# A planner in place of hand-set rates for the first two stages, and 32x32 squares turned by VectorE

## The chip, the cores and the metric

One core of a Trainium2 chip runs the whole program. The metric is the device time of one execution in microseconds (us). The engines are TensorE (PE, its weight loads PEld), VectorE (DVE), ScalarE (ACT), GpSimd (POOL, unused here) and SyncE (SP), whose queue issues every DMA.

## What is computed

```python
scale = 1.0 / np.sqrt(D)                                   # B, H, S, D = 8, 8, 512, 64; 32 state rows
a  = softmax(scale * x @ state.T);  xread = a  @ state     # per batch and head
a2 = softmax(scale * state @ x.T);  sread = a2 @ x
x = concat([xread, sread], rows).reshape(4352, 512)        # heads side by side
h = ((x @ w1) * (x @ w2)) @ w3 @ w_out                     # 512 -> 1024 -> 1024 -> 512
h = h @ w_in; out = (h - tanh(h)) @ w_out2                 # 512 -> 2048 -> 512
```

The weights come as 64-bit floats and are unpacked on the chip; a product is made of three passes over operands split in a high and a low half.

## The kernel before

A block is one batch: 512 tokens. Blocks 0 to 7 are `xread`, block 8 holds the 256 `sread` rows of all batches. There are four stages, and attention beside the first two.

- **Weights** (`startup`, L551, and what it calls). `w3` and `w_out` are loaded and unpacked: ScalarE makes two instructions of a piece (L153, L154), VectorE three (L161 to L170). `w3` is turned on TensorE (`w_ps`), split (`w3t`) and multiplied with `w_out` into `w3o` (L540). `w1` and `w2` are unpacked in four pairs (`w12_pair`, tiles `raw`, `dt`, `w`).
- **Fold** (L613). The state of four batches times a pair of `w1`, `w2` gives `m`: 16 folds for each half of the batches. ScalarE copies it to `fe`, which goes to DRAM (`mdr`); `load_m` (L648) fetches it block by block as `mq`, and `unfold` (L658) splits it on ScalarE and VectorE into `m`. So stage 1 multiplies the softmax `at` with `m` and needs no `xread`.
- **Attention** (`attn_steps`, L299), for each block: `x` is loaded row by row (`xn`, L293), turned on TensorE in four groups of four 128x128 transposes (`xt_ps`) and copied by ScalarE; scores (L314) are made for tiles of 64 rows; they are turned again (`sm_ps`) so that the 32 scores of a row lie side by side for the first softmax, and after it a third time (`at_ps`). The second softmax goes through `et_ps` and the `sr` matmuls (L379).
- **Stage 1** (L667): two groups `ab_ps` of six matmuls for each of 8 slices k, whose product is split into `ph`. **Stage 2** (L700): `y_ps` adds up over k and goes to DRAM.
- **Stages 3 and 4** (from L846) read `y` back and are left as they are.

The order of the work is written out by hand: a loop over (b, k) calls stage 1 two slices ahead of stage 2, and after each call `point()` (L202) adds parts of attention, folds and unpacking at rates such as 0.58 or 0.5 a call; the start has its own table of digits, `STARTUP` (L37). Every engine runs its instructions in the order in which they were written. PSUM has four work banks in turn, one pool tag `ps`.

Of the kernel before, what the change touches and what calls it, by code (L numbers as in the profile page):

```python
# [18 lines left out]
P = 128  # L19
# [24 lines left out]
def tile_kernel(  # L44
# [31 lines left out]
    pw = ctx.enter_context(tc.tile_pool(name="pw", bufs=4, space=PSUM))  # L76
# [16 lines left out]
        (r, kk): dram.tile([2, 4 * P, 512], F32, name=f"mdr{r}_{kk}")  # L93
# [7 lines left out]
    def ps(name):  # L101
        return pw.tile([P, 512], F32, tag="ps", name=name)
# [56 lines left out]
    def unpack_vector(t):  # L159
        tf = t.bitcast(F32)  # L160
        nc.vector.tensor_scalar(  # L161
            out=tf, in0=tf, scalar1=EXP_LO, scalar2=EXP_HI, op0=ALU.max, op1=ALU.min
        )
        nc.vector.tensor_scalar(
            out=t, in0=t, scalar1=3, scalar2=0x3FFFFFFF,
            op0=ALU.logical_shift_left, op1=ALU.bitwise_and,
        )

    def unpack_end(raw, t):
# [4 lines left out]
        return t.bitcast(F32)  # L174


    jobs = []

    def background():
        if jobs and next(jobs[0], True):  # L180
            jobs.pop(0)

    def drain():
        while jobs:
            background()

    owed = {"major": 0.0, "job": 0.0, "fold": 0.0}
    rate = dict(owed)

    def pay(major, fold, job):  # L190
        for _ in range(major):
            if turned[0] <= limit[0]:
                todo.major()
                todo.minor()
        for _ in range(fold):
            if folds:
                folds.pop(0)()
                settle()
        for _ in range(job):
            background()  # L200

    def point():  # L202

        settle()
        todo.minor()
        due = []
        for k in ("major", "fold", "job"):
            owed[k] += rate[k]
            due.append(int(owed[k] + 1e-6))
            owed[k] -= due[-1]  # L210
        pay(*due)

    folds = []

    turned, limit = [0], [1]

    class Stream:


        def __init__(self, parts):  # L220
            self.parts, self.mark = parts, None
            self.move()

        def move(self):
            self.mark = next(self.parts, None)

        def minor(self):
            if self.mark is False:
                self.move()

        def major(self):
            while self.mark is False:
                self.move()
            settle()
            if self.mark:
                self.move()

        def until(self, seen, key):
            while key not in seen:
                self.major()  # L240
# [17 lines left out]
    with ExitStack() as actx:  # L258
# [18 lines left out]

        def turn_state(r):
# [18 lines left out]


        def attn_steps(b):  # L299
            s = {}  # L300
            bb = b % 4

            def xt(q):
                t = ps(f"xt_ps{b}_{q}")
                transposes(t, [xn[b][:, c, q * P:(q + 1) * P] for c in range(NC)])
                s["xt", q] = pt.tile([P, 512], F32, tag="xt", name=f"xt{b}_{q}", bufs=4)
                copy(s["xt", q], t)

# [22 lines left out]
            def soft(g):
                t = ps(f"sm_ps{b}_{g}")
                sc = s["sc", g]
                transposes(t, [sc[:, c * P:(c + 1) * P] for c in range(NC)])
                r2 = pt.tile([P, 1], F32, tag="r2", name=f"r2{b}_{g}", bufs=2)
                nc.scalar.activation(sc, sc, AF.Exp, bias=s["m2", g], scale=SCALE, accum_out=r2)
                t3 = t.rearrange("p (a n) -> p a n", n=NS)
                na = 512 // NS
                m = pt.tile([P, na], F32, tag="m1", name=f"m1{b}_{g}", bufs=2)
                nc.vector.tensor_reduce(out=m, in_=t3, axis=AX.X, op=ALU.max)  # L340
                a = pt.tile([P, na, NS], F32, tag="xt", name=f"a{b}_{g}", bufs=4)
# [642 lines left out]
```

## Time and profile before

| | |
|---|---|
| median of 3 runs | 1408.23 us (1404.87 to 1409.86) |
| profiled execution | 1408.06 us, its span 1406.2 us |
| TensorE busy | 1312.6 us, 93% |
| VectorE busy | 943.7 us, 67% |
| ScalarE busy | 787.1 us, 56% |
| mean granted TensorE clock | 0.971 |
| DMA | 124.87 MB, 28.6% of 16 engines |

The span runs from the first to the last instruction; 1.9 us lie around it. Shares are means over stages that differ, so the rows below are cut by stretch. A releaser is who ended a wait. Matmuls overlap, so the step from one start to the next says more than a duration.

### The profile page before, as it was taken

The page shows a single profiled execution, that of the slowest core. Times are in us where ns is not written, and L with a number is a line of the kernel's source. Part 1 is how long each engine was busy: PE and PEld are TensorE (multiplying, and loading weights), DVE is VectorE, ACT ScalarE, POOL GpSimd, SP SyncE. Part 2 cuts the span into 40 slices and gives each one's busy share as a digit, 9 for nine tenths or more (in the row PEclk, how much of TensorE's full clock was granted, in tenths as well). Part 3 has the DMA queues.
Part 4 walks back from the last instruction along what each step waited for, and adds up shares of the span by engine and source line. Part 5 has one row for each costly group of instructions (what it writes and reads, how often), then busy time and mean ns, then how long its engine had stood idle before and what let it go on. Part 6 is the DMA issues. An engine that isn't in the chain of part 4 may idle for free.

```text
span 1406.2 us, 17414 instructions
## 1 busy us (share of the span) xinstructions
PE 1312.6 (93%) x6608; PEld 1058.3 (75%) x6608; DVE 943.7 (67%) x1573; ACT 787.1 (56%) x1269; POOL 0.7 (0%) x6
## 2 busy tenths in 40 slices
PE   5865798999899899999999999999999999999997
PEld 3653576767677687987888888888888888888886
DVE  6674445564566655246998768777687776877776
ACT  8956645677665654245655545455454544545454
POOL 0000000000000000000000000000000000000000
PEclk9987799999999999999999999999999999999999
DMA  9717344477765631134301010010100101001000
GB/s 301 244 61 209 90 123 140 136 225 241 209 187 146 183 105 53 53 128 138 117 0 61 0 42 19 1 61 0 60 0 1 60 1 60 0 1 45 1 31 16
DMA packets 92780, 124.87 MB, mean 89 GB/s; under 512 B 41240, under 2 KB 54552, under 8 KB 90648
## 3 DMA queue, kind: packets, MB, share of 16 engines
q1 hardware_dynamic: 92696, 123.76, 28.6%
q8 instruction: 52, 0.85, 0.3%
q14 instruction: 32, 0.26, 0.1%
HBM read 80.74 MB, written 42.99 MB: 88 GB/s over the span
## 4 chain that ended last, share of the span: by engine, by line
PE 72%; ACT 10%; DVE 9%; DMA 4%; issue 2%; SPq 2%; ACTq 0%; DVEq 0%
PE o_ps L903 25%; PE h_ps L141 24%; PE ab_ps L141 11%; PE y_ps L708 9%; DMA mdr<-fe 2%; ACT raw_p L154 1%; ACT fe L111 1%; SPq L632 1%; DMA raw_p<-in_moe_w_dram 1%; ACT raw_w L154 1%; PE m_ps L622 1%; DMA ydr<-y 1%; DVE a L343 1%; DVE m L114 1%; PE sr_ps L379 1%
## 5 line engine op out<-in xcount | busy, mean ns | idle before, releaser
L141 PE MATMUL h_ps<-yt,w2in 128*128 128x512 f32 (+1 forms) x1728 | 394.0, 377 | 0.0
L141 PEld LDWEIGHTS h_ps<-yt,w2in 128*128 128x128 f32 x1728 | 313.4, 188 | 61.2
L141 PE MATMUL ab_ps<-at,m 128*128 128x512 f32 x768 | 213.2, 413 | 25.5 <-ACT m L111 18.1
L708 PE MATMUL y_ps<-ph,w3o 128*128 128x512 f32 (+1 forms) x864 | 218.6, 390 | 0.0
L141 PEld LDWEIGHTS ab_ps<-at,m 128*128 128x128 f32 x768 | 143.4, 195 | 68.6 <-ACT m L111 21.4
L708 PEld LDWEIGHTS y_ps<-ph,w3o 128*128 128x128 f32 x864 | 155.6, 191 | 34.6 <-issue 4.6
L111 ACT ACTIVATE ph<-ac 128x512 fp32r<-128x512 f32 (+1 forms) x72 | 43.8, 609 | 131.7 <-DVE ac L695 131.7
L114 DVE TENSOR_TENSOR m<-mq,m 128x512 fp32r<-128x512 f32 x64 | 44.2, 690 | 83.2 <-ACT m L111 83.2
L114 DVE TENSOR_TENSOR ph<-ac,ph 128x512 fp32r<-128x512 f32 (+1 forms) x72 | 47.7, 663 | 48.7 <-ACT ph L111 48.7
L695 DVE TENSOR_TENSOR ac<-ab_ps,ac 128x512 f32<-128x512 f32 (+1 forms) x72 | 47.4, 658 | 45.2 <-PE ab_ps L141 45.1
L111 ACT ACTIVATE ac<-ab_ps 128x512 f32<-128x512 f32 (+1 forms) x72 | 42.3, 587 | 34.8 <-PE ab_ps L141 30.1
L540 PE MATMUL w3o_ps<-wo,w3t 128*128 128x512 f32 x192 | 55.6, 443 | 5.0 <-ACT w3t L111 3.4
L622 PE MATMUL m_ps<-w,uu 64*128 64x512 f32 x192 | 39.2, 515 | 14.3 <-ACT w L111 5.9
L540 PEld LDWEIGHTS w3o_ps<-wo,w3t 128*128 128x128 f32 x192 | 39.8, 216 | 15.1 <-ACT w3t L111 3.9
L111 ACT ACTIVATE fe<-m_ps 128x512 f32<-128x512 f32 x64 | 34.8, 599 | 23.5 <-DMA mdr<-fe 15.8
L154 ACT ACTIVATE raw_w<-raw_w 128x512 uint16<-128x512 uint32 x32 | 43.7, 1364 | 1.0
L622 PEld LDWEIGHTS m_ps<-w,uu 64*128 64x128 f32 x192 | 22.5, 233 | 28.4 <-ACT w L111 6.5
L111 ACT ACTIVATE m<-mq 128x512 fp32r<-128x512 f32 x64 | 40.8, 637 | 0.0
L133 PE MATMUL w_ps<-ident,dt_p 128*128 128x128 f32 x64 | 12.0, 318 | 30.1 <-DVE dt_p L170 30.1
L913 DVE COPY ob<-o_ps 128x512 f32<-128x512 f32 x17 | 11.8, 692 | 38.6 <-PE o_ps L903 38.6
L111 ACT ACTIVATE ob<-o_ps 128x512 f32<-128x512 f32 x17 | 10.2, 599 | 44.9 <-PE o_ps L903 44.9
L133 PEld LDWEIGHTS w_ps<-ident,dt_p 128*128 128x128 f32 x64 | 8.2, 159 | 34.5 <-issue 23.5
(1812 smaller groups left out, 2353.8 us busy)
## 6 DMA issues: line engine op xcount, KB each, us to landing
mdr<-fe SPq DMA_DIRECT2D x128, 128.0 KB, 2.5
mq<-mdr SPq DMA_DIRECT2D x64, 256.0 KB, 4.5
xn<-in_x_dram SPq DMA_DIRECT2D x32, 256.0 KB, 5.0
raw<-in_moe_w_dram SPq DMA_DIRECT2D x16, 512.0 KB, 8.6
ydr<-y SPq DMA_DIRECT2D x32, 256.0 KB, 3.5
raw_w<-in_moe_w_in_dram SPq DMA_DIRECT2D x16, 512.0 KB, 4.5
raw_w<-in_moe_w_out_dram SPq DMA_DIRECT2D x16, 512.0 KB, 4.2
yr<-ydr SPq DMA_DIRECT2D x8, 1024.0 KB, 4.8
```

The source lines that it names most:

```text
L111: nc.scalar.activation(dst, src, AF.Copy)
L114: nc.vector.tensor_tensor(out=lo, in0=src, in1=hi.bitcast(F32), op=ALU.subtract)
L133: nc.tensor.transpose(dst[:, i * P:(i + 1) * P], s, ident)
L141: nc.tensor.matmul(out_ap, lhs(i), rhs(j), start=(n == 0), stop=(n == m - 1))
L154: nc.scalar.activation(tail, w[:, :, 0], AF.Copy, scale=TAIL)
L343: nc.vector.tensor_tensor(out=a, in0=t3, in1=mb, op=ALU.subtract)
L379: nc.tensor.matmul(t[q * NS:(q + 1) * NS], s["e2t", j][:, c, q * NS:(q + 1) * NS], xn[b][:, c, h * D:(h + 1) * D], start=(c == 0), stop=(c ...
L540: nc.tensor.matmul(acc[a], v[:, i, a * P:(a + 1) * P], wo[j // 2][:, l, (j % 2) * 512:(j % 2) * 512 + 512], start=(j == 0 and e == 0), sto ...
L622: nc.tensor.matmul(ts[j].rearrange("p (k f) -> p k f", k=2), uu[r][d, i, q * P:(q + 1) * P], w[d, :, l, q, :], start=(n == 0), stop=(n == ...
L695: nc.vector.tensor_tensor(out=pf, in0=t, in1=pf, op=ALU.mult)
L708: nc.tensor.matmul(acc[o][:, :n], w3o[k // 2][:, i, c + o * P:c + (o + 1) * P], p[:, j], start=(k == 0 and e == 0), stop=(k == NK - 1 and ...
L903: nc.tensor.matmul(acc[t], g[:, i, t * P:(t + 1) * P], w[:, l, c], start=(f == 0 and e == 0), stop=(f == NF - 1 and e == 2),)
```

## The change

All of the work up to stage 2 is cut into parts. A part names its engine, an estimated duration, what it needs, what it makes, and which slots of which ring it takes and gives. `Plan.run` goes through streams of parts and writes the part that can start first, or one of better rank within 250 ns of it; so the order of every queue comes from the plan. The digits, rates, `point`, `pay` and the generator of attention go. The four PSUM banks get a tag each, which the plan picks. What the parts do changes at these places:

- `x` is loaded a second time as `xb`, in eight DMAs of 32 rows, laid out by head; VectorE turns its 32x32 squares into `xt` (four instructions a block). The state is loaded a second time too (`zb`) and turned the same way (`ut`). Scores are made of tiles of 32 rows, twice as many, adding up in pairs. `by_head` turns the scores in squares in place of `sm_ps`, `back` turns them back in place of `at_ps`. `et_ps` stays on TensorE.
- Folds: for blocks 0 to 3 ScalarE copies one half and VectorE the other; for blocks 4 to 7 the high and the low half are made at the fold and both stored, so `m` is loaded whole, without a split.
- `load_m` takes four DMAs of 32 rows; the ring `m` has three slots, `mq` is gone.

```diff
-STARTUP = (
-    "0000000000010101010101011011011011",
-    "0000000000000000122222222222222222",
-)
+class Plan:
+    NEAR = 250.0
+    REACH = {"PE": 200.0, "ACT": 130.0, "DVE": 130.0, "SP": 0.0}
...
+    def emit(self, p, t):
+        end = t + p["dur"]
+        self.free[p["eng"]] = end
+        if p["bytes"]:
+            self.moved = max(self.moved, t + 600) + p["bytes"] / 300.0
+            end = self.moved + 1600
+        reach = end + self.REACH[p["eng"]]
...
+            t0, _, _, _, p0 = min(can, key=lambda c: c[0])
+            t, _, parts, k, p = min(
+                (c for c in can if c[4]["eng"] == p0["eng"] and c[0] <= t0 + self.NEAR),
+                key=lambda c: (c[1], c[0]),
+            )
+            del parts[k]
+            self.emit(p, t)
...
+        def band(q, j):
+            q = (q + 2 * j) % KT
+            return slice(q * NS, (q + 1) * NS)
...
+        def load_xb(b):
+            if b < B:
+                xb[b] = pt.tile([P, G, 4, NC, D], F32, tag="xb", name=f"xb{b}")
+                for j in range(G):
+                    for q in range(KT):
+                        nc.sync.dma_start(
+                            xb[b][band(q, j), j].rearrange("p g c d -> p g (c d)"),
+                            x[b, 2 * q + j].rearrange("(g p c) d -> p g (c d)", p=NS, c=NC),
+                        )
...
-            def xt(q):
-                t = ps(f"xt_ps{b}_{q}")
-                transposes(t, [xn[b][:, c, q * P:(q + 1) * P] for c in range(NC)])
-                s["xt", q] = pt.tile([P, 512], F32, tag="xt", name=f"xt{b}_{q}", bufs=4)
-                copy(s["xt", q], t)
+            def xt(j, e):
+                t = pt.tile([P, 512], F32, tag="xt", name=f"xt{b}_{j}{e}", bufs=4)
+                nc.vector.transpose(
+                    out=t.rearrange("p (c g i) -> p g c i", c=NC, g=4),
+                    in_=xb[b][:, j, :, :, e * NS:(e + 1) * NS],
+                )
...
+                for e in range(2):
+                    for q in range(KT):
+                        for j in range(G):
+                            d = band(q, j)
+                            nc.tensor.matmul(
+                                s["ps", j][q * NS:(q + 1) * NS],
+                                ut[b // 4][d, j, bb, e], s["xt", j, e][d],
+                                start=(e == 0), stop=(e == 1), tile_position=(d.start, q * NS),
+                            )
...
+            def by_head(j):
+                s["a", j] = pt.tile([P, 512], F32, tag="xt", name=f"a{b}_{j}", bufs=4)
+                nc.vector.transpose(out=s["a", j], in_=s["sc", j])
...
+            def back(j):
+                s["at", j] = pt.tile([P, 512], F32, tag="sc", name=f"at{b}_{j}", bufs=2)
+                nc.vector.transpose(out=s["at", j], in_=s["a", j])
...
+        def fold_whole(kk, q, j):
+            src, f = fold_half(0, kk, q, j, 1)
+            if j == 0:
+                copy(f, src)
+            else:
+                nc.vector.tensor_copy(f, src)
...
-                    mq[b, k] = pa.tile([P, 512], F32, tag="mq", name=f"mq{b}_{k}", bufs=3)
-                    nc.sync.dma_start(mq[b, k], mdr[r, k // 2][k % 2, bb * P:(bb + 1) * P])
+            mt[b, k] = pa.tile([P, 2, 512], F32R, tag="m", name=f"m{b}_{k}", bufs=3)
+            for q in range(KT):
+                rows = slice(q * NS, (q + 1) * NS)
+                to = mt[b, k][rows].bitcast(F32)
+                of = mdr[r, k // 2][q, bb * NS:(bb + 1) * NS, k % 2]
+                nc.sync.dma_start(*((to, of) if r else (to[:, 1], of[:, 1])))
```

How the order moves, at three places. In a name like `ab_ps5_2_0_4143` stand block, slice k, half and a buffer number.

TensorE where block 5 starts stage 1 (`xt`, `et` and `sc` belong to the attention of block 6), before:

```order
L708 MATMUL y_ps4_2_3643<-ph4_5_3843,w3o1_183 128x512 x3
L708 MATMUL y_ps4_3_3647<-ph4_5_3843,w3o1_183 128x512 x3
L141 MATMUL ab_ps5_0_0_3984<-at5_3879,m5_0_3958 128x512 x6
L133 MATMUL xt_ps6_0_3993<-ident_74,xn6_3526 128x128 x4
L708 MATMUL y_ps4_0_3610<-ph4_6_3921,w3o1_183 128x512 x3
L708 MATMUL y_ps4_1_3614<-ph4_6_3921,w3o1_183 128x512 x3
L141 MATMUL ab_ps5_0_1_4014<-at5_3879,m5_0_3958 128x512 x6
L133 MATMUL xt_ps6_1_4025<-ident_74,xn6_3526 128x128 x4
```

and after:

```order
L249 MATMUL ab_ps5_1_1_4130<-at5_3992,m5_1_3783 128x512 x6
L249 MATMUL ab_ps5_2_0_4143<-at5_3992,m5_2_3808 128x512 x6
L249 MATMUL ab_ps5_2_1_4162<-at5_3992,m5_2_3808 128x512 x6
L249 MATMUL ab_ps5_3_0_4177<-at5_3992,m5_3_4089 128x512 x6
L241 MATMUL et_ps6_0_4193<-ident_74,sc6_0_4137 128x128 x4
L249 MATMUL ab_ps5_3_1_4201<-at5_3992,m5_3_4089 128x512 x6
L1035 MATMUL y_ps5_0_4219<-ph5_0_4096,w3o0_525 128x512 x3
L1035 MATMUL y_ps5_1_4223<-ph5_0_4096,w3o0_525 128x512 x3
```

The `xt`, `sm` and `at` groups are gone from between the groups of stages 1 and 2, and several slices of stage 1 now follow one another before stage 2 takes them up.

ScalarE ahead of the first half of `m` (block 0, slice 0), in the weights' part; `fe` are copies of folds, `dt12` and `raw12` the unpacking of `w1` and `w2`. Before:

```order
L111 ACTIVATE at0_845<-at_ps0_1_928 128x512
L153 ACTIVATE dt12_2_0_848<-raw12_4_679 128x512
L154 ACTIVATE raw12_4_679<-raw12_4_679 128x512
L111 ACTIVATE fe0_1_0_946<-m_ps0_1_0_0_938 128x2x256
L111 ACTIVATE fe0_1_0_946<-m_ps0_1_0_1_939 128x2x256
L111 ACTIVATE fe0_1_1_962<-m_ps0_1_1_0_954 128x2x256
L111 ACTIVATE fe0_1_1_962<-m_ps0_1_1_1_955 128x2x256
L111 ACTIVATE fe0_1_2_977<-m_ps0_1_2_0_969 128x2x256
L111 ACTIVATE fe0_1_2_977<-m_ps0_1_2_1_970 128x2x256
L111 ACTIVATE fe0_1_3_992<-m_ps0_1_3_0_984 128x2x256
L111 ACTIVATE fe0_1_3_992<-m_ps0_1_3_1_985 128x2x256
L111 ACTIVATE m0_0_999<-mq0_0_921 128x512
```

and after:

```order
L260 ACTIVATE dt12_4_917<-raw12_4_734 128x512
L265 ACTIVATE raw12_4_734<-raw12_4_734 128x512
L219 ACTIVATE w3o1_940<-w3o_ps1_0_546 128x512
L219 ACTIVATE fe0_1_001_943<-m_ps0_1_0_0_922 128x512
L219 ACTIVATE fe0_1_101_955<-m_ps0_1_1_0_947 128x512
L219 ACTIVATE w3o1_940<-w3o_ps1_1_550 128x512
L219 ACTIVATE m0_0_934<-m0_0_934 128x512
```

Of the second pair's folds two copies stand ahead of it now, not eight, and half of `w3o` comes after it.

SP's queue around the fourth load of block 5 (`raw_w2` fetches and `w2dr` stores belong to the last weights, `ydr` stores to stage 2, `xn` to block 7 or 6), before:

```order
L656 DMA mq5_2_3973<-mdr1_1_99 128x512
L147 DMA raw_w2_27_4009<-in_moe2_w_out_dram 128x1024
L656 DMA mq5_3_4032<-mdr1_1_99 128x512
L756 DMA w2dr_in6_114<-dt_w2_25_3981 128x512
L293 DMA xn7_4057<-in_x_dram 128x8x64
```

and after:

```order
L1049 DMA ydr4_89<-y4_1_4026 128x512
L382 DMA xn6_4031<-in_x_dram 128x8x64 x4
L1141 DMA w2dr_in5_112<-dt_w2_21_3893 128x512
L1049 DMA ydr4_89<-y4_2_4042 128x512
L255 DMA raw_w2_23_4059<-in_moe2_w_out_dram 128x1024
L1049 DMA ydr4_89<-y4_3_4047 128x512
L982 DMA m5_3_4089<-mdr1_1_99 32x1024 x4
L391 DMA xb7_4120<-in_x_dram 32x4x256 x8
L982 DMA m5_4_4154<-mdr1_2_100 32x1024 x4
```

A load is now four DMAs of 32 rows, and the second copy of `x` is eight more between two loads.

## Rows read from the trace of the kernel before

**Rows 1.** The page: busy time of an engine, and the DMA queue's packets, MB, share.

```profile
PE 1312.6 (93%) x6608; PEld 1058.3 (75%) x6608; DVE 943.7 (67%) x1573; ACT 787.1 (56%) x1269; POOL 0.7 (0%) x6
...
q1 hardware_dynamic: 92696, 123.76, 28.6%
```

**Rows 2.** Stretches: us, each engine's busy time (instructions), PEclk, DMA share, GB/s.

```profile
0.00:131.00 131.00, 83.42 (x430) 62.07 (x431) 80.14 (x139) 101.49 (x126) 0.70 (x6) 0.88 0.69 211
131.00:209.00 78.00, 64.43 (x336) 46.17 (x336) 39.95 (x75) 44.33 (x76) 0.00 (x0) 0.84 0.41 105
209.00:652.00 443.00, 422.38 (x2486) 333.25 (x2484) 235.14 (x437) 252.29 (x431) 0.00 (x0) 0.98 0.50 149
652.00:1406.00 754.00, 742.41 (x3360) 616.81 (x3358) 588.45 (x924) 388.96 (x637) 0.00 (x0) 1.00 0.09 31
```

**Rows 3.** Who TensorE waited for: total us, times, longest; 0:131, 131:652, 400:560.

```profile
PE w_ps L133 <- DVE dt_p L170: 30.1, 11, 7.3
...
PE m_ps L622 <- ACT w L111: 5.9, 2, 5.5
...
PE ab_ps L141 <- ACT m L111: 7.9, 3, 4.7
```

**Rows 4.** TensorE in order of time: start, us, instructions, [idle before <-releaser].

```profile
130.67 4.90 PE L141 MATMUL ab_ps<-at,m 128*128 128x512 f32 x12 [2.77 <-ACT m L111]
...
429.03 2.93 PE L141 MATMUL ab_ps<-at,m 128*128 128x512 f32 x6 [2.82 <-ACT m L111]
434.32 1.92 PE L141 MATMUL ab_ps<-at,m 128*128 128x512 f32 x6
...
488.40 2.93 PE L141 MATMUL ab_ps<-at,m 128*128 128x512 f32 x6 [4.70 <-ACT m L111]
493.43 0.60 PE L133 MATMUL et_ps<-ident,sc 128*128 128x128 f32 x4
```

**Rows 5.** TensorE in order of time, a dense stretch.

```profile
517.04 1.53 PE L708 MATMUL y_ps<-ph,w3o 128*128 128x512 f32 x6
518.40 0.60 PE L133 MATMUL xt_ps<-ident,xn 128*128 128x128 f32 x4
518.76 1.64 PE L141 MATMUL ab_ps<-at,m 128*128 128x512 f32 x6
520.23 1.54 PE L708 MATMUL y_ps<-ph,w3o 128*128 128x512 f32 x6
...
529.94 1.09 PE L314 MATMUL sc_ps<-xt,uf 64*32 64x512 f32 x16
530.96 1.65 PE L708 MATMUL y_ps<-ph,w3o 128*128 128x512 f32 x6
```

**Rows 6.** ScalarE's groups by form, 0:650: busy us, mean ns.

```profile
L111 ACT ACTIVATE m<-mq 128x512 fp32r<-128x512 f32 x64 | 40.8, 637 | 0.0
...
L111 ACT ACTIVATE fe<-m_ps 128x512 f32<-128x512 f32 x64 | 34.8, 599 | 23.5 <-DMA mdr<-fe 15.8 <-PE m_ps L622 7.6
...
L154 ACT ACTIVATE raw<-raw 128x512 uint16<-128x512 uint32 x16 | 21.7, 1357 | 0.5
...
L111 ACT ACTIVATE xt<-xt_ps 128x512 f32<-128x512 f32 x32 | 19.3, 603 | 2.7 <-PE xt_ps L133 2.5
...
L153 ACT ACTIVATE dt<-raw 128x512 f32<-128x512 f32 x16 | 10.7, 671 | 0.0
```

**Rows 7.** VectorE's groups by form, 0:650.

```profile
L164 DVE TENSOR_SCALAR dt_w<-dt_w 128x512 uint32<-128x512 uint32 x32 | 13.7, 428 | 1.1
...
L343 DVE TENSOR_TENSOR a<-sm_ps,m 128x512 f32<-128x512 f32 x16 | 11.1, 692 | 0.6
```

**Rows 8.** Loads of m: SP's issue (ns min/median/max), landing; landing of 512 KB loads.

```profile
L656 SPq DMA_DIRECT2D mq<-mdr x64: 320/422/2068, 121.2 to 627.4; - x64
DMA to landing us min/median/max: 2.6/4.5/5.9
...
raw<-in_moe_w_dram SPq DMA_DIRECT2D x16, 512.0 KB, 8.6
```

More of the change, by code (lines that the diff above doesn't have):

```diff
@@ L173, in unpack_end, with part, later @@
         )
[L174 to L240, printed above, removed]
+    plan = Plan()
+    for name, n in (
[4 rows of a table added]
+    ):
+        plan.ring(name, n)
+    def part(stream, eng, cost, fn, need=(), make=(), take=(), give=(), size=0, rank=None):
+        if isinstance(cost, tuple):
+            kind, n = cost
+            cost = COST[kind][0] + COST[kind][1] * n
+        stream.append(dict(
+            eng=eng, dur=cost, fn=fn, need=tuple(need), make=tuple(make),
+            take=tuple(t if len(t) == 3 else (*t, 1) for t in take), give=tuple(give), bytes=size, rank=rank,
+        ))
+    def later(f, *v):
+        return lambda: f(*v)
     yt, yr = {}, {}
@@ L331, in soft @@
[L331 to L341, printed above, removed]
-                mb = m.rearrange("p (a o) -> p a o", o=1).to_broadcast([P, na, NS])
-                nc.vector.tensor_tensor(out=a, in0=t3, in1=mb, op=ALU.subtract)
+            na = 512 // NS
@@ new lines, in p, with pe_t @@
+            def p(eng, cost, f, v=(), need=(), make=(), take=(), give=(), size=0):
+                part(
+                    a_s, eng, cost, later(f, *v), [(b, *n) for n in need], [(b, *n) for n in make],
+                    [(t, (b, *k), u) for t, k, u in take], [(b, *g) for g in give], size,
+                    rank=3 if b == 0 and eng != "PE" else None,
+                )
+            full, thin = ("vector", 512), ("vector", 16)
+            small = (("vector", 1),) * 2
+            def pe_t(n):
+                return n * TURN
@@ L468, in tile_kernel @@
[L468 to L486 removed]
+        w12, raws, f32s, acc_w = {}, {}, {}, {}
@@ new lines, in w3_slice @@
+        def w3_slice(h, a):
+            if h not in w3o:
+                w3o[h] = wp.tile([P, 2, 2, 1024], F32R, tag="o", name=f"w3o{h}", bufs=2)
+            c = slice((a % 2) * 512, (a % 2) * 512 + 512)
+            o = w3o[h][:, a // 2]
+            return acc_w[h, a], o[:, 0, c], o[:, 1, c]
+        for i in range(nj + nj // 2):
+            if i < nj:
+                for half in range(2):
+                    part(
+                        w_s, "SP", 450, later(fetch, i, half), (), [("raw", i, half)], (), (), 1 << 19
+                    )
@@ L719, in tile_kernel, with y_take, y_store @@
-        blocks = list(range(B - 1)) + [B, B - 1]
-        steps = [(b, k) for b in blocks for k in range(NK)]
-        def first(i, h):
-            if i < len(steps):
-                stage1(*steps[i], h)
+        ys = {}
+        def y_take(b, o, n):
+            pool, tag = (px, ("th", "z")[o % 2]) if b == B - 1 else (pa, "y")
+            ys[b, o] = pool.tile([P, 512], F32, tag=tag, name=f"y{b}_{o}")[:, :n]
+            copy(ys[b, o], acc[o][:, :n])
+        def y_store(b, o):
+            nc.sync.dma_start(ydr[b][:, o, :], ys[b, o])
```

1107 lines of the change are left out of this document (707 added, 400 removed), and 4 rows, old and new, of the table plan.

## Prediction

> **What bounds the kernel now.** I read the page's first part, then a table of stretches. TensorE is busy 93% of the span [rows 1], but not evenly. From 652 us on (stages 3 and 4) it is busy 742.4 of 754 us at full clock; before that it stands still for 47.6 us in the first 131, 13.6 in the next 78 and 20.6 in the 443 after [rows 2]. So the first 652 us are where something can be won: 82 us of idle time, and a granted clock of 0.88, 0.84 and 0.98. Then I asked who TensorE waits for. In the first stretch it is the unpacking of the weights (30.1 us for `dt_p`); later it is ScalarE's halves: `w` 5.9 us, and `m` 7.9 us in three waits between 400 and 560 us [rows 3]. In the list in order of time, stage 1 first starts at 130.67 us; two of the three `m` waits are followed by matmuls at the lower clock, 2.93 us for a group that takes 1.36 otherwise [rows 4, 5]. VectorE and ScalarE are busy 355 and 398 us of the 652, the DMA engines at half [rows 2]: nobody else is near its end on average. The waits are chains between engines whose order is fixed in advance.
>
> The sum is made against the profiled execution, 1408.06 us (span 1406.2), which is 0.2 us off the median of 1408.23. What 0.3% (4 us) does not exceed I call no change.
>
> **Part 1: transposes leave TensorE.** Per block 4 `xt`, 2 `sm` and 2 `at` groups go, 64 in all. The price of one is read from a dense stretch: a y group starts at 517.04, `xt` at 518.40, the next ab group at 518.76 and y at 520.23. From `xt` to that y are 1.83 us, where a group without it takes 1.36 (517.04 to 518.40): 0.47 us each [rows 5]. Sixteen of them lie in the first two stretches, 48 in the third: 48 x 0.47 = 22.6 us off TensorE's path there. Bounds: 0.36 us (start to start alone), so 17.3; and 0.60 (the duration written beside it), so 28.8.
>
> Added: each score matmul of 64 rows becomes two of 32. Now a block's 16 records take 1.02 us, from 529.94 to 530.96 [rows 5]; the new ones are twice as many, on eight places of the array as before, so I take 2.04 us, and 6 x 1.02 = 6.1 us for the six blocks of the third stretch. Bounds: 0 to 6.1. [...]
>
> **Part 2: VectorE turns squares.** 64 + 2 transposes of 128x512, which no row shows. Bounds: 0.43 us (the cheapest 128x512 row of VectorE) and 1.36 (the slowest row of that size, ScalarE's) [rows 6, 7]; I take 0.69, the row of an instruction that reads one tile and writes another at one element at a time: 45.5 us. Sixteen fold copies move to it as well (11 us). So 355 + 57 = 412 us of some 592: hidden beside TensorE. At 1.36 it would be 456, still less than TensorE's work. What it costs is delay in a block's softmax chain, and a block is turned well ahead of its use.
>
> **Part 3: ScalarE is relieved.** Gone are 32 `xt` copies (0.603), 16 fold copies (0.599) and 32 `m` halves of blocks 4 to 7 (0.637) [rows 6]: 49 us of 398. For blocks 4 to 7 nothing stands any more between the landing of `m` and its matmul. The three waits of 7.9 us lie in that part [rows 3], and the two slow restarts cost 434.32 - 429.03 and 493.43 - 488.40 where 2.72 is usual: 2.6 and 2.3 us [rows 4]. Together -12.8.
>
> **Part 4: the first stretch.** ScalarE sets it: 101.5 us busy of 131 [rows 2], and its order up to the first `m` half can be counted. Ahead of it go 10 fold copies (6.0), 4 `xt` copies (2.4), one copy of the turned state and two of `w3o` (1.8) and one unit of unpacking (0.67 + 1.36) [rows 6]; one copy of 128x128 comes ahead. -12.0 us, all on the path: stage 1 would start at 119. Bounds: 0, if VectorE, which gets eight transposes and six copies there (80.1 us busy plus 9.7), becomes the end of the chain; -27, if the new order also fills half of the 29.5 us in which ScalarE is not busy.
>
> **Part 5: 131 to 209 us.** Of 78 us, 13.6 are idle and 64.4 x 0.16 = 10.3 are lost to the clock [rows 2]. One block's eight transposes (-3.8) go, its scores cost +1.0. The weights' second half, waited for here [rows 3], is unpacked with fewer fold copies ahead of it on ScalarE; I take half of the 24 lost: -11. Sum -14; bounds 0 and -26.
>
> **Part 6: loads of `m`.** Before, a load had a ring of three and the split a ring of two. Now one ring of three holds both, four DMAs fill a tile, and for blocks 4 to 7 it is twice as large. A load can be issued when the third pair before it has run. From the order, with 1.36 us a group, I summed TensorE's work between that pair and the pair that needs the tile: at least 9.1 us for the 29 tiles of blocks 0 to 3, at least 7.5 for the 32 of blocks 4 to 7. Needed are 4 x 0.42 us of issue, 4.5 to land [rows 8], and in blocks 0 to 3 the two halves (0.64 + 0.69) and some 1.3 behind other instructions: 8.8 and 6.2 us. So nothing is late if landing stays at 4.5. If it grows by 2 us the shortfalls add up to 8 us, by 4 to 35, by 6 to 73. DMA traffic grows: 403 issues become 643, all on SP's queue, and by their shapes 123.8 MB [rows 1] become 149.4, all 25.7 more before 652 us. There it was 102 MB (211, 105 and 149 GB/s over their stretches, [rows 2]); now 127.5 MB in some 592 us, 215 GB/s, about what the first stretch ran at. I take +2 us on landing: +8. Bounds: 0, and +36 with the 8.6 us that a 512 KB load took in the crowded start [rows 8].
>
> **Part 7: the rest of the order.** In the third stretch 20.6 - 7.9 = 12.7 us of idle and 8.9 - 4.9 = 4 us of clock are left. The plan places each part when its inputs and slots are free, with 226.7 ns for a matmul, which the row bears out (1.36 / 6). I take -12 of these 16.7; bounds 0 and -16.7.
>
> Stages 3 and 4 keep their order: 0.
>
> **Sum.** -12.0 (part 4), -14 (part 5), and in the third stretch -22.6 + 6.1 - 12.8 + 8 - 12 = -33.3; together -59.3: 1408.06 - 59.3 = 1348.8, so **1348 us**. Each term at its good end gives some -112 (1296), at its bad end about +12 (1420).
>
> **Rivals.**
> - *The plan packs nearly everything.* Parts 4, 5 and 7 at their good ends, no late load: -27 - 26 - 22.6 + 6.1 - 12.8 - 16.7 = -99, 1309 us. For it: the durations in the plan for ScalarE and VectorE are near or above the rows. Against: an order fixed in advance never meets all durations. 0.18.
> - *Landing becomes as in the start*, 8.6 us: +36 in place of +8, 1377 us. For it: 25% more bytes in less time, and mean traffic of a crowded stretch. 0.16.
> - *Late loads take over (slower).* Same mechanism further on: past +6 us of landing, that is 10.5 us, the shortfalls (73) eat the whole gain; at +7 they are some 103, 1348 - 8 + 103 = 1443 us. For it: tiles filled from 32 rows at a time, SP's queue that stops at the first DMA that must wait, so a store behind a load waits with it. Against: the longest landing of an `m` load seen is 5.9 us [rows 8]. 0.08. [...]
> - *The work leaves but the time stays*: parts 4, 5 and 7 give nothing, as new waits replace the old: 1408 - 22.6 + 6.1 - 12.8 + 8 = 1387 us. 0.05.
>
> **How the numbers follow.** The forecast (1325 to 1370) has 0.53. The range from 1303 to 1395 takes in the packing case, the start-like landing and the staying idle time, leaving out the slower case and the best and worst corners, under 0.2. Of the late loads and of the staying time 0.01 each ends within 0.3%: 0.02. Faster by over 0.3%: 0.53 + 0.18 + 0.16 + 0.04 = 0.91; slower 0.07.
>
> **What would show it.** Stage 1 starts near 119 us and stage 3 near 592 (652 now). A turned square lasts 0.69 us; the scores of a block 2.04. No wait for an `m` half in blocks 4 to 7. Granted clock above 0.9 from 131 us on. Wrong would be: landing of `m` over 8 us with TensorE waiting for that DMA; VectorE as the one it waits for; or stages 3 and 4 longer than 754 us.

## The result and the profile after

The changed kernel takes 1347.18 us (median of 4 runs, 1344.34 to 1352.87), the kernel before 1406.55 in the same comparison: ratio 0.958, 95% interval 0.954 to 0.963. The profiled execution took 1345.59 us, its span is 1343.8. The forecast was 1348. By the medians the change is worth 59.4 us, between the two profiled executions 62.5; the forecast was 59.3.

The page's first part (busy us, share of the span, instructions) and its row on the DMA queue, against [rows 1]:

```profile
PE 1284.6 (96%) x6480; PEld 1028.5 (77%) x6480; DVE 985.7 (73%) x1655; ACT 743.1 (55%) x1187; POOL 0.7 (0%) x6
...
q1 hardware_dynamic: 123160, 149.46, 37.3%
```

The stretches up to the start of stage 1, to the start of stage 3 and to the end; columns as in [rows 2]:

```profile
0.00:116.03 116.03, 83.45 (x407) 58.24 (x408) 88.58 (x152) 91.35 (x108) 0.70 (x6) 0.90 0.78 230
116.03:591.84 475.81, 459.23 (x2713) 353.02 (x2714) 311.64 (x583) 264.88 (x446) 0.00 (x0) 0.98 0.75 215
591.84:1343.80 751.96, 741.91 (x3361) 617.24 (x3359) 585.53 (x921) 386.91 (x635) 0.00 (x0) 0.99 0.08 28
```

and the same stretches of the kernel before:

```profile
0.00:130.67 130.67, 83.09 (x430) 61.74 (x430) 79.81 (x139) 101.16 (x126) 0.70 (x6) 0.88 0.69 211
130.67:651.80 521.13, 486.94 (x2819) 379.56 (x2820) 275.43 (x511) 296.83 (x507) 0.00 (x0) 0.96 0.48 142
```

Of the 60.0 us that stage 3 starts earlier, 27.4 are TensorE's busy time (570.0 to 542.7) and 32.6 its idle time (81.8 to 49.2). Stages 3 and 4 gave 2.4 more.

TensorE's waits after, from the start of stage 1 to stage 3 (us, times, longest):

```profile
PE ab_ps L249 <- ACT sc L219: 3.3, 1, 3.3
PE ab_ps L249 <- ACT ac L219: 2.4, 3, 1.2
PE m_ps L885 <- DVE fe L908: 2.1, 1, 2.1
...
PE ab_ps L249 <- DMA m<-mdr: 1.7, 1, 1.7
...
PE ab_ps L249 <- DVE m L222: 0.4, 1, 0.4
...
PE ab_ps L249 <- ACT m L219: 0.3, 1, 0.3
```

The first row of this view for the kernel before, between 116 and 592 us, is

```profile
PE ab_ps L141 <- ACT m L111: 18.1, 8, 4.7
```

So from the start of stage 1 on the waits for `m` halves are nearly gone, those for `w` (5.9 in [rows 3]) too, and nothing of their size has come instead. Ahead of stage 1 it is otherwise. The 30.1 us for `dt_p` [rows 3] are down to 7.3, but TensorE now waits for the halves of `wo`, which it did not do there before (0 to 116 us):

```profile
PE w3o_ps L731 <- ACT wo L219: 9.5, 7, 1.8
PE w_ps L241 <- DVE dt_p L283: 7.3, 1, 7.3
...
PE w3o_ps L731 <- DVE wo L222: 4.1, 6, 1.1
```

What VectorE's turned squares and TensorE's score tiles cost (groups by form, 0 to 592 us):

```profile
L403 DVE STREAM_TRANSPOSE xt<-xb 128x512 f32<-128x512 f32 x32 | 20.5, 684 | 0.0
...
L486 DVE STREAM_TRANSPOSE at<-a 128x512 f32<-128x512 f32 x16 | 11.4, 710 | 0.8
L428 DVE STREAM_TRANSPOSE a<-sc 128x512 f32<-128x512 f32 x16 | 11.3, 705 | 2.7 <-ACT sc L219 2.7
```

```profile
185.73 1.95 PE L416 MATMUL sc_ps<-xt,ut 32*32 32x512 f32 x32
187.60 0.96 PE L885 MATMUL m_ps<-w,uu 64*128 64x512 f32 x6
```

The loads of `m`: landing of all of them, against 4.5 us in [rows 8], then SP's time to issue one (ns), then their two sizes (KB each, median us to landing):

```profile
DMA to landing us min/median/max: 1.9/3.0/6.8
```

```profile
L982 SPq DMA_DIRECT2D m<-mdr x256: 302/419/1541, 110.0 to 563.2; - x128
```

```profile
m<-mdr SPq DMA_DIRECT2D x128, 128.0 KB, 3.9
...
m<-mdr SPq DMA_DIRECT2D x128, 64.0 KB, 2.5
```

These are pieces, four to a tile. From the first issue on, a whole tile takes three more issues of 0.42 us, an estimate of 3.8 us for blocks 0 to 3 (256 KB, which was one DMA of 4.5 us before) and 5.2 us for blocks 4 to 7 (512 KB).

### The profile page after: what moved, and what is told of

Same layout as the page of the kernel before. It is cut to its first block, busy times and chain, and to the rows that moved or that the text cites. A ratio compares the mean times of both kernels' runs of the same rounds, so it can differ in the third digit from the quotient of the medians.

```text
span 1343.8 us, 17703 instructions
## 1 busy us (share of the span) xinstructions
PE 1284.6 (96%) x6480; PEld 1028.5 (77%) x6480; DVE 985.7 (73%) x1655; ACT 743.1 (55%) x1187; POOL 0.7 (0%) x6
## 4 chain that ended last, share of the span: by engine, by line
PE 77%; DVE 6%; DMA 6%; ACT 6%; SPq 3%; issue 2%; DVEq 0%; ACTq 0%
PE h_ps L249 26%; PE o_ps L1294 26%; PE ab_ps L249 10%; PE y_ps L1035 9%; PE w3o_ps L731 2%; PE m_ps L885 1%; DMA m<-mdr 1%; DMA raw_w<-in_moe_w_out_dram 1%; ACT raw_p L265 1%; SPq L982 1%; DMA raw_w<-in_moe_w_in_dram 1%; DMA raw_p<-in_moe_w_dram 1%; DMA mdr<-fe 1%; ACT dt_p L260 0%; SPq L391 0%
## 5 line engine op out<-in xcount | busy, mean ns | idle before, releaser
L249 PE MATMUL ab_ps<-at,m 128*128 128x512 f32 x768 | 196.1, 406 | 10.8 <-ACT sc L219 3.3
L1035 PE MATMUL y_ps<-ph,w3o 128*128 128x512 f32 (+1 forms) x864 | 201.0, 382 | 0.2 <-DVE ph L222 0.2
L222 DVE TENSOR_TENSOR ph<-ac,ph 128x512 fp32r<-128x512 f32 (+1 forms) x72 | 47.5, 659 | 82.8 <-ACT ph L219 81.8
L731 PE MATMUL w3o_ps<-wo,w3t 128*128 128x512 f32 x192 | 63.6, 482 | 18.4 <-ACT wo L219 9.5
L731 PEld LDWEIGHTS w3o_ps<-wo,w3t 128*128 128x128 f32 x192 | 42.9, 233 | 36.2 <-ACT wo L219 11.3
L219 ACT ACTIVATE ac<-ab_ps 128x512 f32<-128x512 f32 (+1 forms) x72 | 40.5, 563 | 12.8 <-PE ab_ps L249 12.7
L1304 DVE COPY ob<-o_ps 128x512 f32<-128x512 f32 x17 | 11.8, 691 | 39.1 <-PE o_ps L1294 39.1
L885 PE MATMUL m_ps<-w,uu 64*128 64x512 f32 x192 | 33.8, 443 | 4.5 <-DVE fe L908 2.1
L260 ACT ACTIVATE dt_w<-raw_w 128x512 f32<-128x512 f32 x32 | 21.5, 671 | 24.7 <-DMA raw_w<-in_moe_w_in_dram 12.2
L219 ACT ACTIVATE ob<-o_ps 128x512 f32<-128x512 f32 x17 | 10.2, 599 | 45.1 <-PE o_ps L1294 45.1
L222 DVE TENSOR_TENSOR m<-m 128x512 fp32r<-128x512 f32 x32 | 21.8, 683 | 16.6 <-ACT m L219 16.5
L219 ACT ACTIVATE m<-m 128x512 fp32r<-128x512 f32 x32 | 20.2, 635 | 22.9 <-DMA m<-mdr 22.9
L219 ACT ACTIVATE fe<-m_ps 128x512 fp32r<-128x512 f32 (+1 forms) x48 | 27.9, 599 | 7.3 <-DMA mdr<-fe 4.3
L885 PEld LDWEIGHTS m_ps<-w,uu 64*128 64x128 f32 x192 | 17.4, 192 | 18.0 <-issue 7.6
L265 ACT ACTIVATE raw_p<-raw_p 128x1024 uint16<-128x1024 uint32 (+1 forms) x14 | 30.5, 2179 | 0.4
## 6 DMA issues: line engine op xcount, KB each, us to landing
m<-mdr SPq DMA_DIRECT2D x128, 128.0 KB, 3.9
xb<-in_x_dram SPq DMA_DIRECT2D x64, 128.0 KB, 3.6
```

The costliest lines, as they stand in the source:

```text
L219: nc.scalar.activation(dst, src, AF.Copy)
L222: nc.vector.tensor_tensor(out=lo, in0=src, in1=hi.bitcast(F32), op=ALU.subtract)
L249: nc.tensor.matmul(out_ap, lhs(i), rhs(j), start=(n == 0), stop=(n == m - 1))
L731: nc.tensor.matmul(acc[a], v[:, i, a * P:(a + 1) * P], wo[j // 2][:, l, (j % 2) * 512:(j % 2) * 512 + 512], start=(j == 0 and e == 0), sto ...
L885: nc.tensor.matmul(ts[j].rearrange("p (k f) -> p k f", k=2), uu[r][1][d, i, q * P:(q + 1) * P], w[d, :, l, q, :], start=(n == 0), stop=(n ...
L1035: nc.tensor.matmul(acc[o][:, :n], w3o[k // 4][:, k // 2 % 2, i, c + o * P:c + (o + 1) * P], p[:, j], start=(k == 0 and e == 0), stop=(k == ...
```

## The experiments

All twelve start from the changed kernel (e7 to e9 from e2). Times are medians of 4 runs; the ratio is to the kernel before, timed in the same comparison, with its 95% interval. "Stage 1" and "stage 3" are the starts of their first matmul, "busy" and "idle" TensorE's time up to stage 3, from each run's own trace.

In every run but e3 the edit also makes the plan write another order. What an order alone can be worth shows where the parts are the same: e1 and e6 lie 17.8 us apart, e2 and e7 13.8, the changed kernel and e10 0.5. So a difference of some 10 us between two kernels is what an edit and its new order do together, not the price of the edit.

| kernel | us | ratio | stage 1 | stage 3 | busy | idle |
|---|---|---|---|---|---|---|
| before | 1406.6 | 1 | 130.7 | 651.8 | 570.0 | 81.8 |
| changed | 1347.2 | 0.958 (0.954-0.963) | 116.0 | 591.8 | 542.7 | 49.2 |
| e1 turns on TensorE | 1385.9 | 0.986 (0.984-0.988) | 128.9 | 630.6 | 568.8 | 61.8 |
| e2 split after load | 1343.3 | 0.955 (0.952-0.958) | 115.7 | 590.5 | 536.9 | 53.6 |
| e3 squares twice | 1372.3 | 0.975 (0.971-0.978) | 122.2 | 620.5 | 554.5 | 66.0 |
| e4 equal durations | 1469.4 | 1.045 (1.042-1.047) | 130.1 | 643.3 | 554.7 | 88.6 |
| e5 squares twice, planned | 1364.1 | 0.970 (0.968-0.972) | 121.5 | 615.1 | 550.5 | 64.7 |
| e6 e1, window 125 | 1368.1 | 0.973 (0.971-0.975) | 135.3 | 613.2 | 556.1 | 57.1 |
| e7 e2, other ranks | 1329.5 | 0.945 (0.942-0.947) | 120.1 | 576.3 | 536.6 | 39.8 |
| e8 e2, third buffer | 1334.1 | 0.948 (0.946-0.950) | 128.0 | 581.5 | 538.7 | 42.8 |
| e9 e2, turn ahead | 1332.1 | 0.948 (0.946-0.950) | 109.9 | 578.6 | 533.8 | 44.8 |
| e10 window 175 | 1347.7 | 0.960 (0.957-0.962) | 127.2 | 592.5 | 543.6 | 49.0 |
| e11 ring of two | 1357.5 | 0.967 (0.965-0.969) | 115.9 | 603.9 | 542.2 | 61.7 |
| e12 fold copies on ScalarE | 1358.5 | 0.966 (0.963-0.970) | 127.4 | 604.9 | 546.0 | 58.9 |

**e1 and e6: the plan without the squares.** `xt`, `by_head` and `back` become parts of TensorE with the copies they had, `xb` and `zb` go, `xn` gets two buffers.

```diff
-                p("DVE", full, by_head, (j,), [("sc", j)], [("a", j)], [("xt", ("a", j), 1)])
+                p("PE", pe_t(4), by_head, (j,), [("sc", j)], [("a", j)], [("ps", ("sm", j), 1)])
...
-                    "DVE", full, back, (j,), [("et", j)], [("back", j)],
+                    "PE", pe_t(4), back, (j,), [("mul1", j)], [("back", j)],
```

> The changed kernel, with its plan kept, but x, scores and softmax are turned by TensorE through PSUM as before (64 quads, with their copies), x is loaded once and the scores are 64-row tiles again. Theory (the sum's terms): 64 x 0.47 = 30 us of transposes come back on TensorE and 8 x 1.02 = 8 us of scores go, ScalarE gets 32 + 2 copies back: some 22 us slower than the changed kernel, near 1370 us. Rival A (the squares are nearly all of the gain): near 1395 us or more. Rival B (the plan alone does it, TensorE's own work is not what counts): within 6 us of the changed kernel, 1341 to 1353 us.

Measured 1385.9, between the theory and rival A: in this order the squares are worth 38.7 us, and the rest of the change, which e1 keeps (the plan, the new folds, the loads in four pieces), 20.6. TensorE's busy time is back at 568.8 us. Of its longest waits the first is new (1.7 us in the changed kernel), the second is there too (9.5):

```profile
PE ab_ps L249 <- DMA m<-mdr: 11.2, 2, 7.1
PE w3o_ps L703 <- ACT wo L219: 9.8, 7, 2.0
```

e6 has the same parts and `NEAR = 125.0`:

> As e1 (turns on TensorE in the plan), with the plan's window for choosing by rank set to 125 ns in place of 250, which makes another order of the same parts. Of e1's 38.7 us over the changed kernel 26.0 are TensorE's busy time and 12.6 its idle time, 11.2 of that two waits for a load of m. Theory (the idle part is this order's own): those waits go, 1365 to 1376 us. Rival (the idle part belongs to the turns on TensorE: more copies on ScalarE, PSUM banks held longer): 1381 to 1390 us.

1368.1 us, as the theory gave it, but not by its mechanism, for the wait stayed:

```profile
PE ab_ps L249 <- DMA m<-mdr: 10.4, 1, 10.4
```

Idle time fell by 4.7 us only; 12.7 are busy time, of the same 3248 matmuls and transposes, at a granted clock of 0.96 (the column after POOL) in place of 0.95:

```profile
0.00:630.60 630.60, 568.83 (x3248) 439.07 (x3249) 364.23 (x668) 375.55 (x587) 0.70 (x6) 0.95 0.63 191
```

```profile
0.00:613.21 613.21, 556.11 (x3248) 434.50 (x3249) 362.07 (x668) 374.39 (x587) 0.70 (x6) 0.96 0.66 196
```

So in these two orders the squares are worth 21 to 39 us and the rest of the change 21 to 38, of 59.4 together; the forecast's 64 x 0.47 - 8 x 1.02 = 22 is at the low end. What the plan is worth without the new folds and loads was not measured.

The wait for a load of `m` is not a slow load. In e6 the load is issued at 412.80 us, right behind stores of folds (`mdr<-fe`), and 5.45 us later TensorE goes on:

```profile
410.89 1.86 SPq L887 DMA_DIRECT2D mdr<-fe  x3
412.80 6.60 SPq L954 DMA_DIRECT2D m<-mdr  x12
```

```profile
418.25 8.57 PE L249 MATMUL ab_ps<-at,m 128*128 128x512 f32 x30 [10.37 <-DMA m<-mdr]
```

The load needs what these stores write. The last of the 96 stores leaves at 319.2 us in the changed kernel and at 412.2 in e6 (425.3 in e1):

```profile
L915 SPq DMA_DIRECT2D mdr<-fe x96: 512/564/1621, 100.5 to 319.2; - x96
```

```profile
L887 SPq DMA_DIRECT2D mdr<-fe x96: 512/519/1144, 101.0 to 412.2; - x96
```

So with the turns on TensorE the folds of blocks 4 to 7 come late in both orders, and stage 1 runs into them. Late folds are not the turns' alone: e12, with the turns on VectorE, stores its last fold at 400.2 us, and no load of `m` is waited for there. What holds the folds back in e1 and e6 (TensorE's own work, ScalarE's copies or the ranks) is not shown.

**e2: the halves of `m` after the load again.** The fold of blocks 4 to 7 is copied whole, `load_m` loads one half for all blocks, and

```diff
-                if b < 4:
+                if True:
```

puts the two halves of each `m` in the plan for all blocks.

> The changed kernel, but blocks 4 to 7 get m as one word and split it after the load, as blocks 0 to 3 do (32 more ScalarE copies, 16 + 16 fold copies in place of 32 + 32 halves, half the bytes stored and loaded for these blocks). Theory (part 3 of the sum: -12.8 us for waits on these halves): about 13 us slower, 1360 us, with waits of TensorE for the halves of m between 330 and 560 us of 5 us or more. Rival: the plan places the copies ahead of their use anyway, as it does for blocks 0 to 3: within 4 us of the changed kernel, and TensorE waits for the halves of m under 2 us in all.

1343.3 us: not slower (the intervals overlap). TensorE waits for the halves of all eight blocks as long as the changed kernel does for four:

```profile
PE ab_ps L249 <- DVE m L222: 0.4, 1, 0.4
...
PE ab_ps L249 <- ACT m L219: 0.3, 1, 0.3
```

The rival holds: it is not the missing halves that took the `m` waits away. The kernel before says the same, for 10.1 of its 18.1 us lie ahead of 400 us, in blocks 0 to 3, which keep both halves in the changed kernel, and they went too:

```profile
PE ab_ps L141 <- ACT m L111: 10.1, 5, 3.9
```

That the plan's order did it is the likely reading; no run has the old order with the other changes.

**e3 and e5: is VectorE hidden?** Each turned square is done twice, `for _ in range(2):`; in e3 in the same order, in e5 with doubled durations in the plan.

> The changed kernel in the same order, but each of VectorE's 64 turns of x, scores and softmax is done twice (64 x 0.69 = 44 us more of VectorE). Theory (turned squares lie beside TensorE's work; VectorE is busy 400 of 592 us): up to 8 us slower, from the 8 turns ahead of stage 1 (8 x 0.69 = 5.5 us), 1347 to 1355 us. Rival (VectorE is the end of the chains): 20 to 44 us slower, 1367 to 1391 us, with TensorE waiting for VectorE.

> As e3, each turned square done twice, but now the plan knows that such a part lasts twice as long and may order the rest around it. Theory (corrected after e3: VectorE's own work is on the path): e3 lost 25 us to 44 us more of VectorE; if it is the work, the new order keeps most of it, 1364 to 1375 us. Rival (e3 lost because its fixed order was made for other durations): 1347 to 1357 us.

e3 lost 25.2 us, in the rival's range, and e5, reordered, still 16.9, at the edge of its theory's, for 43 and 44 us more of VectorE. The stretch up to stage 3 of e3 has VectorE (third number) at 443 of 620 us, and TensorE (first) at a clock of 0.95:

```profile
0.00:620.46 620.46, 554.49 (x3121) 414.22 (x3121) 443.13 (x798) 357.14 (x553) 0.70 (x6) 0.95 0.72 208
```

One of the places in e3, TensorE in order of time, where `at` of a block comes late:

```profile
432.34 0.50 PE L249 MATMUL ab_ps<-at,m 128*128 128x512 f32 x1 [3.23 <-ACT at L219]
```

The same wait is 1.00 us in the changed kernel. In the 4 us up to 432 TensorE is busy 1.11 us; from this matmul on its granted clock (the column after POOL) is 0.61:

```profile
428.00:432.00 4.00, 1.11 (x5) 0.56 (x3) 3.72 (x10) 0.60 (x2) 0.00 (x0) 1.00 0.82 216
432.34:436.00 3.66, 3.40 (x8) 2.44 (x9) 3.59 (x8) 1.69 (x4) 0.00 (x0) 0.61 1.23 285
```

Of the 28.6 us to stage 3, 16.8 are idle time and 11.8 busy time of the same instructions. VectorE is not busy all the time; a late softmax chain or a late `ac` reaches TensorE in pieces of 1 to 3 us (in all 6.1 us for ScalarE's `ac`, 4.4 for VectorE's and 3.2 for `at`; 2.4, 1.1 and 1.0 in the changed kernel). The doubled turns load VectorE and also make every softmax chain longer; these runs do not tell the two apart.

**e4: a plan without durations.**

```diff
             cost = COST[kind][0] + COST[kind][1] * n
+        cost = 700.0 if cost else 0
```

> The changed kernel, but its plan takes every part to last 700 ns (needs, slots and ranks are kept): the order then follows from needs and ranks alone. Theory (part 7 of the sum: the plan packs because its durations are near those of the rows): 20 us or more slower, 1367 us or more, with new waits of TensorE in the stretch from block 1 to stage 3. Rival (needs, slots and ranks do it, the durations hardly count): within 8 us, 1339 to 1355 us.

1469.4 us, 122 slower than the changed kernel and 4% slower than before. Of these, 51 us lie ahead of stage 3. The rest is behind it: ScalarE is still unpacking the second layer's weights when stage 3 begins (at 643 us, and still at 711), and TensorE waits for what stands behind them in ScalarE's queue:

```profile
PE o_ps L1295 <- ACT g(0, 0)_5820 L219: 48.7, 1, 48.7
PE h_ps L249 <- ACT yt L219: 17.5, 2, 9.9
```

**e11: two buffers for `m`.** `("m", 2)` and `bufs=2`.

> The changed kernel with two buffers for m in place of three. Part 6 of the sum took 6.5 us for a load of m to land and counted 8 us of late loads; one pair less between the freed buffer and its next use (2 x 1.36 us of TensorE's work at least) would make some 60 tiles short by about 2.7 us more each. By that: over 60 us slower, 1410 us or more, with TensorE waiting for loads of m. Rival (loads land in 3.0 us, as the changed kernel's trace shows, so two buffers nearly do): 1350 to 1368 us.

1357.5 us: 10 slower, with waits of 6.2 us for the ScalarE half of `m` and 3.6 for its loads:

```profile
PE ab_ps L249 <- ACT m L219: 6.2, 4, 4.6
PE ab_ps L249 <- DMA m<-mdr: 3.6, 3, 1.7
```

The rival holds: with loads that land this early (3.0 us in the changed kernel), two buffers nearly do.

**e12: the fold copies back on ScalarE.**

```diff
-                                f_s, *(("ACT", ("scalar", 512)), ("DVE", ("vector", 512)))[j],
+                                f_s, "ACT", ("scalar", 512),
```

> The changed kernel, but all 32 copies of the first folds are ScalarE's, as before (16 go back from VectorE). Theory (part 4: ScalarE sets the start of stage 1, and 10 such copies ahead of it are 6.0 us of it): stage 1 starts at 122 us or later, in place of 116.0, and what it loses there stays: 1352 to 1358 us. Rival (the start is later, but stages 1 and 2 have room and catch up): stage 1 starts at 122 us or later and the time is 1343 to 1351 us.

1358.5 us: 11.3 slower, stage 1 at 127.4. That is at the upper edge of the theory's range (by 0.5 us outside) and far from the rival's. But the start itself is not what costs, as e10 shows with the same late start and no loss. Here TensorE waits 7.3 us for ScalarE's `ac` and 6.3 for `sc`:

```profile
PE ab_ps L249 <- ACT ac L219: 7.3, 7, 2.1
```

```profile
127.38 5.49 PE L249 MATMUL ab_ps<-at,m 128*128 128x512 f32 x12 [6.32 <-ACT sc L219]
```

The changed kernel has 2.4 and 3.3. The 11.3 us are those of the copies and of the new order together.

**e7 to e10: other orders.** e10 changes one number, `NEAR = 175.0`.

> The changed kernel with one number of its plan changed: the window for choosing by rank is 175 ns in place of 250; the same parts in another order. The plan's own clock ends stage 2 at 564 us (571). Theory (the plan's clock sees it, some 21 us early): 1340 us (1335 to 1344). Rival (such a number moves the chip's time by chance only): outside that, on either side.

No change, 1347.7 us, with stage 1 starting 11 us later: the theory missed and the rival holds. The plan's clock is not good to 7 us.

e7 keeps e2's parts and changes the window and the ranks of ten of the twelve streams (two of them shown):

```diff
-    NEAR = 250.0
+    NEAR = 150.0
...
-        s2 = plan.stream({"PE": 2.5, "ACT": 0.5, "SP": 1}, 24)
+        s2 = plan.stream({"PE": 5.5, "ACT": -1.0, "SP": 2}, 24)
...
-        u_s = plan.stream({"ACT": 6, "DVE": 6, "SP": 5})
+        u_s = plan.stream({"ACT": 12.0, "DVE": 6.5, "SP": 6.0})
```

> e2 (blocks 4 to 7 split after the load) with other ranks of the streams and a window of 150 ns, taken because the plan's own clock ends stage 2 at 557 us with them, against 568 for e2 and 571 for the changed kernel. The chip ended stage 2 at 592, 631 and 590 us where the plan's clock said 571, 612 and 568: 21, 19 and 23 us later. Theory (the plan's clock sees what counts): stage 3 starts at 578 us, the time is 1331 us (1326 to 1337). Rival (what the plan's clock gains the chip does not: loads, clock of TensorE): 1341 to 1348 us.

1329.5 us, stage 3 at 576.3: the theory holds, and this is the fastest kernel measured, 0.945 of before. It runs as many matmuls and transposes on TensorE as e2; idle time fell from 53.6 to 39.8 us, busy time stayed (536.9 and 536.6).

```profile
0.00:576.32 576.32, 536.55 (x3121) 410.33 (x3122) 408.79 (x750) 366.49 (x569) 0.70 (x6) 0.97 0.68 195
```

e8 and e9 aimed at the first stretch, where 32.6 of the changed kernel's 49.2 idle us lie. e8 has `("pdt", 3), ("praw", 3)`, e9 a stream of its own for the turns of w3:

```diff
+        z_s = plan.stream({"PE": 4.3, "ACT": 2, "DVE": -4.0}, 40)
...
-                x_s, "PE", 4 * TURN, later(w3_turn, t), whole[:1], [("w3x", t)],
+                z_s, "PE", 4 * TURN, later(w3_turn, t), whole[:1], [("w3x", t)],
```

> e2 with a third buffer for the unpacked w3/w_out tiles in the first stretch (the second half of w3 is loaded in tiles of 128 columns to make room) and other ranks, window 175 ns; the plan's own clock ends at 557 us. In the changed kernel ScalarE waits for VectorE's last use of such a tile five times in the first 50 us (0.84 to 1.56 us each) and TensorE 13.6 us in all for the wo halves. Theory (those waits are the two buffers): they go, stage 1 starts by 110 us, the time is 1331 us (1324 to 1337). Rival (ScalarE's 91 us of work ahead of stage 1 sets it, buffers or not): stage 1 starts at 114 us or later, 1335 to 1347 us.

> e2 with the turning of w3 (and its two halves) in a stream of its own, so that TensorE turns tile t+1 ahead of the matmuls of tile t; the plan takes 320 and 240 ns for a w3 matmul and 150 for a fold's in place of 226.7 and 128, and has other ranks and a window of 150 ns. In e7 TensorE waits 17.5 us in all between a turn and its matmuls in the first stretch (9.3 + 4.3 for ScalarE's wo and w3t, 2.8 + 1.1 for VectorE's), and eleven w3 matmuls take 4.3 us there, where 2.6 is the least seen. Theory (those waits are the order turn, matmuls, turn, matmuls on TensorE): the waits for wo and w3t fall under 9 us, the time is 1320 us (1313 to 1325). Rival (ScalarE's work sets the first stretch, so the waits only move): stage 1 starts no earlier than 118 us, 1326 to 1334 us.

e8 took 1334.1 us, in the range of its theory but not by its mechanism: stage 1 starts at 128.0, not by 110, and TensorE still waits 10.8 us for ScalarE's half of `wo`, so a third buffer alone does not remove these waits (e8 has other ranks too). e9 took 1332.1 us, outside its theory and in the range of its rival, though its stage 1 starts earlier than that rival allows. The waits for `wo` and `w3t` fell as the theory said, and nearly the same time is now waited one step earlier, for the unpacking:

```profile
PE w_ps L241 <- DVE dt_p L283: 20.5, 8, 7.3
...
PE w3o_ps L732 <- ACT wo L219: 2.3, 1, 2.3
```

(The first is 7.3 us in one wait in the changed kernel.) The stage 1 of e9 starts 10.2 us before e7's and its stage 3 starts 2.3 us after. What would shorten the first stretch stays open.

## Why the prediction was right, and where its steps were not

The total, the sign and both marks fit: stage 1 at 116.0 (119 forecast), stage 3 at 591.8 (592), no wait of size for an `m` half, VectorE's square at 0.684 to 0.710 us (0.69), a block's scores at 187.60 - 185.73 = 1.87 us (2.04), stages 3 and 4 at 752 (754). Up to stage 1 the change gave 14.6 us (12.0 forecast), from there to stage 3 45.3 (47.3). But several terms were right in sum and wrong by themselves.

- **Part 1** (TensorE's work). Busy time up to stage 3 fell by 27.4 us: the count of transposes less scores (-22 at the forecast's prices) and some of the clock (granted 0.97 up to stage 3, 0.94 before). The scores came out by the row: twice the records took 1.87 us where half of them took 1.02 [rows 5], so on eight places the smaller tiles gave little. That the added half costs nothing, the 0 at that term's good end, no run shows: it took 0.85 us a block (1.87 - 1.02).
- **Part 2** had the busy sum (400 of 592 us; 412 forecast) and the duration (0.684 to 0.710 us; 0.69) right. Its "hidden beside TensorE" is not borne out: another 43 us of such squares cost 17 to 25 us (e3, e5). The 57 us added here were probably not free either, but their own price was not measured, only the net gain of the turns.
- **Part 3** had the size of the waits and not their mechanism: "For blocks 4 to 7 nothing stands any more between the landing of `m` and its matmul" credits 12.8 us to the halves that go. The waits did go, 18.1 to 0.3 us, but in blocks 0 to 3 as well, and e2 puts the halves back and loses nothing. That leaves the order in which the plan writes a half ahead of its use, as the likely cause. The fold copies, listed in the same part, may count for more: 11.3 us in e12, its other order included.
- **Part 4** gave the size (ScalarE's busy time up to stage 1 fell from 101.2 to 91.4 us) but "all on the path" is not shown: e10 starts stage 1 at 127.2 and loses nothing, e9 starts it at 109.9 and gains nothing over e7.
- **Part 5** cannot be read by itself: its stretch has no counterpart in the new order. From the start of stage 1 on only the sum with parts 1, 3, 6 and 7 can be compared.
- **Part 6** failed at "I take +2 us on landing: +8". A piece landed in 3.0 us with more traffic, and a whole tile, by the estimate above, in 3.8 or 5.2 us from its first issue, where part 6 counted 6.2 without growth and 8.2 with it. TensorE waited 1.7 us in all for these loads, so the rivals on late loads had no ground. Whether the slope behind them was right is not shown, for e11 took a buffer away while loads landed early. SP's queue did stop at a DMA that had to wait, as one of them has it (in the changed kernel it issued nothing from 531.4 to 545.25 us, when a load of `m` had waited 13.8 us for `ab_ps`).
- **Part 7** was the plan, and too small if part 3's gain is the plan's as well. That the durations carry it is shown by e4, that "an order fixed in advance never meets all durations" by e10, where the plan's clock gained 7 us and the chip none. The case "packs nearly everything" (1309) did not come, but e7 went nearly half of the way, 18 of 39 us, with fewer bytes and another order.

That 1348 stood so close to 1347.18 is partly luck. Without the +8 that did not come, the sum would have been 1341, so the other terms together were too good by some 6 us; part 2, which put VectorE's work at nothing, is a candidate, not shown. And the four runs themselves lie between 1344 and 1353.

## What to carry to other kernels

Put a part back before crediting it: where a scheduler reorders everything, a wait that vanishes says nothing of which edit removed it, and one order is not enough to price a part. Work beside the path is not free merely because its engine is only two thirds busy (VectorE here, 400 of 592 us, and 43 us more cost 17 to 25); double it once and see what that costs. And judge an order by TensorE's idle plus slowed time up to the next dense stage, not by when one stage begins.

## What was not expected of the hardware

The same instructions of TensorE do not take the same time in two orders: 3248 of them were busy 568.8 us in e1 and 556.1 in e6, at granted clocks of 0.95 and 0.96. The sum of idle time does not settle which it will be: the kernel before stood still 20 us longer than e1 and was busy only 1.2 us longer, and e7 stood still 13.8 us less than e2 and was busy as long. In the first stretch of the changed kernel eleven `w3o` matmuls come several times, each time behind two short waits for the halves of `wo` (the second wait shown; the first is 1.21, 1.21 and 1.20 us):

```profile
18.11 4.38 PE L731 MATMUL w3o_ps<-wo,w3t 128*128 128x512 f32 x11 [0.31 <-DVE wo L222]
...
25.64 4.29 PE L731 MATMUL w3o_ps<-wo,w3t 128*128 128x512 f32 x11 [1.00 <-DVE wo L222]
...
32.38 2.83 PE L731 MATMUL w3o_ps<-wo,w3t 128*128 128x512 f32 x11 [0.31 <-DVE wo L222]
```

The granted clock of just these stretches (the column after POOL) is 0.61, 0.62 and 1.00:

```profile
18.11:22.49 4.38, 4.38 (x13) 3.42 (x14) 3.08 (x4) 4.35 (x3) 0.00 (x0) 0.61 1.05 377
25.64:29.93 4.29, 4.29 (x13) 3.38 (x14) 1.99 (x3) 3.63 (x2) 0.00 (x0) 0.62 1.04 385
32.38:35.21 2.83, 2.83 (x13) 2.28 (x14) 1.39 (x2) 2.80 (x2) 0.00 (x0) 1.00 0.48 126
```

The first and the third stand behind the same pair of waits, and one ran at a granted clock of 0.61 and took 4.38 us, the other at 1.00 and took 2.83. What a short wait costs beyond itself is therefore not shown by its length.

And the cost of a load in pieces: one DMA of 32 partitions landed in 2.5 us (64 KB) or 3.9 us (128 KB) while the queues moved 215 GB/s, where one of 256 KB over 128 partitions had taken 4.5 us at 149 GB/s [rows 2, 8]. Four pieces of 64 KB bring a tile of 256 KB no later than that one DMA did (3.8 us by the estimate above).
